# Where the MLP's gate is multiplied in: prepared second weights and sums instead of each pair's results

## The chip, the cores and the metric

The kernel runs on one core of a Trainium2 chip. The metric is device time in microseconds (us) of one launch. The engines named below are PE (TensorE, the matrix products), ACT (ScalarE), DVE (VectorE), POOL (GpSimd) and SP (SyncE, which issues most transfers). Each engine takes its instructions in the order in which they are written; between engines there are only waits on what an instruction reads or overwrites.

## What is computed

A transformer block for 2048 tokens of 640 values with adaptive layer norm: a modulation row is made from `c`, then come linear attention and an MLP. The part that matters is the last line but one, where the row `gb` (640 values, one for each output column) scales the MLP's output:

```
sa, ca, ga, sb, cb, gb = (silu(c) @ w_mod) in six rows of 640
x = x + ga * attention(layernorm(x) * (1 + ca) + sa)
h = layernorm(x) * (1 + cb) + sb
r = relu(h @ w1 + b1)                  # 640 -> 1728
x = x + gb * ((r * r) @ w2 + b2)       # 1728 -> 640
```

Because `gb` scales columns, `gb * (r2 @ w2)` is the same as `r2 @ (w2 * gb)`.

## The kernel before

**Tiles.** Tokens go in 8 pairs j = 0..7 of two 128-token tiles. The hidden axis of 1728 is 14 chunks f (the last one 64 wide), taken two at a time as n = 0..6. A round (j, n) has two halves: `up(j, 2n)` and `up(j, 2n+1)`, each 15 products of 256 columns, and between them the two parts of the `down` products of the round before it. PE works in fp32r; every operand is a rounded high part (ACT copies it, "hi") and a low part (DVE subtracts, `lo`, line 87), and a product is three matmuls (`three`, line 83).

**The chain beside PE.** `up` ends with a relu on ACT (line 1235) and a square on DVE (line 1236). After the second half `split_a` makes the hi (ACT, lines 1259 and 1265) and lo (DVE) parts of the squared chunk pair, and the next round's `down` reads them.

**Second weights.** Pairs 0 and 1 (`PLAIN` = 2) multiply with the plain chunks `W2[f]`. They are prepared by three lists in the same order, `p_load`, `p_hi`, `p_lo`: load a raw row tile by SP (line 994), round it on ACT (line 1001), subtract on DVE (line 1006, by `lo`). W1 and W2 chunks alternate. The first nine entries of the list are rounded during the attention's output stage (j = 1 to 6 there), the other nineteen in the twelve halves of rounds (0, 0) to (0, 5), as many a half as `PREPS` says: 1, 3, 2, 1, 2, 2, 1, 2, 1, 1, 1, 2 (`prep`, line 1450, at lines 1534 and 1585). W2 chunks 2 to 13 are among the nineteen.

**Sums.** From pair 2 on, `down_pair` uses seven products in place of eight, on sums and differences of blocks. The weights' sums are made once, during pair 1 and the start of pair 2: `t_load(n)` loads two raw chunks again, `t_sums(n)` (line 1300) makes five differences on DVE, `t_split(n)` (line 1314) rounds four pieces on ACT, subtracts on DVE and stores three of them to DRAM, from where POOL fetches them in a ring for each later pair. The last pair uses plain chunks again for its last rounds; `plain_load` and `plain_split` (lines 1331 and 1335) prepare a part of two of them anew.

**The gate.** `gb_b` holds `gb` on all partitions. For pairs 0 and 1, `end` (line 1418) multiplies each of four pieces of the accumulated result by it, from PSUM into a row tile. For pairs 2 to 6, `gate` (line 1425) multiplies each finished row tile, 128x640, in place; for pair 7, line 1567 does so before the last products, and `last_downs` (line 1433) multiplies the four pieces that come last into a scratch tile and adds them. `finish` adds the residual and stores.

**What sets the order.** All of it stands in `manual_schedule` blocks for PE, DVE, ACT and POOL: the order on an engine is the order of the text. In the main loop (line 1506) a first half is `up(j, 2n)`, `down` part 0, `layer` (the next pair's layer norm and its transposes, `t2`), `t_split`, `prep`; then `up(j, 2n+1)`, `split_a`, `down` part 1, `prep`, `end`, `layer`, `t_sums`, `t_load`.

Of the kernel before, what the change touches and what calls it, by code (L numbers as in the profile page):

```python
# [8 lines left out]
F32 = mybir.dt.float32  # L9
# [3 lines left out]
ALU = mybir.AluOpType  # L13
AX = mybir.AxisListType

P = 128
S = 2048
D = 640
# [19 lines left out]
PLAIN = 2  # L38
# [12 lines left out]
def kernel(  # L51
# [19 lines left out]
    nc = tc.nc  # L71
# [99 lines left out]
    gb_b = const.tile([P, D], F32, name="gb_b")  # L171
# [224 lines left out]
    def proj(nm, t, between=None):  # L396
        p = pj(f"p{nm}{t}")
        j, i = divmod(t, 2)
        s = slice(i * P, (i + 1) * P)
        for h, (a, b) in enumerate(CUT):  # L400
            terms = []
            for d in range(NC):
                w = W[nm, d]
                terms += three(HT[j][:, d, 0, s], HT[j][:, d, 1, s], w[:, 0, a:b], w[:, 1, a:b])
            at, hook = 0, None
            if between and h == between[0]:
                at, hook = between[1:]
                mm(p[h][:, : b - a], terms[:at], last=False)
                hook()
            mm(p[h][:, : b - a], terms[at:], first=(at == 0))  # L410
        return p
# [299 lines left out]
    for t in range(2, NT - 2):  # L711
        j, i = divmod(t, 2)
# [13 lines left out]
        p = proj("v", t, (1, 0, lambda: t1(j + 1, 4)) if t == NT - 3 else None)  # L726
# [269 lines left out]

    RAW, RAWT, EARLY_ROWS = {}, [], 3

    def prep_hi(k, f):
        w = (W1 if k == "1" else W2)[f]  # L1000
        nc.scalar.activation(w[:, 0], RAW[k, f], AF.Copy)
# [12 lines left out]
    preps = [("1", f) for f in range(EARLY)]  # L1014
# [2 lines left out]
        preps += [("2", f + 1)] * (f + 1 < NF) + [("1", EARLY + f)] * (EARLY + f < NF)  # L1017
    assert len(preps) == 2 * NF
    places = []
    todo = {"load": list(preps), "hi": list(preps), "lo": list(preps)}  # L1020

    def p_load(n=1):
        for _ in range(n):
            if todo["load"]:
                k, f = todo["load"].pop(0)
                prep_load(k, f, places[k, f](f"w{k}_{f}"))

    def p_hi(n=1):
        for _ in range(n):
            if todo["hi"]:  # L1030
                prep_hi(*todo["hi"].pop(0))
# [14 lines left out]
    def load_x1(j):  # L1046
        load_xm(j)
        load_xx(j)
# [16 lines left out]
    def add_x(j, *tiles):  # L1065
        for i in tiles:
            nc.vector.tensor_tensor(XM[j][:, i], XM[j][:, i], XX[j][i], op=ALU.add)
            nc.sync.dma_start(X1[j][:, i], XM[j][:, i])
# [13 lines left out]
    NB = NT // 2  # L1082
# [40 lines left out]
    for j in range(NB):  # L1123
        nxt = j + 1 < NB
        b, c = 2 * j + 5, 2 * j + 6
        late_te = j == 0
        te_at = (0, 1) if 0 < j < 6 else (1, 2)
        if j == 4:
            load_x1(0)
        if j < 5:  # L1130
            p_load()
        if j != 5:
            e_prod(b)
        e_recip(b - 1)
        e_scale(b - 1)
        if j == 5:
            q_chain(KEPT + 3, False)
            add_x(0, 0, 1)
            nc.vector.tensor_tensor(bb, b2s[0], gb_b, op=ALU.mult)
            ln0 = ln_parts(XM[0], "b0")  # L1140
        load_e(b + 2)
        def te(at):
            for i, gs in enumerate((range(3), range(3, NG))):
                if nxt and not late_te and te_at[i] == at:
                    tr_e(j + 1, gs)

        do_wo(j, 0, 0)
        te(0)
        if j == 5:
            exps(EQ[KEPT + 3])  # L1150
            q_sums(KEPT + 3)
            e_prod(b)
        do_wo(j, 0, 1)
        if j == 7:
            t2(0, 0)
            t2(0, 1)
        te(1)
        if j == 5 or j == 6:
            next(ln0)
        if j in SUMS:  # L1160
            q_sums(KEPT + SUMS[j])
        e_prod(c)
        e_recip(b)
        e_scale(b)
        if j in SPREAD:
            q_chain(KEPT + SPREAD[j], False)
        do_wo(j, 1, 0)
        if j == 7:
            t2(0, 2)
            t2(0, 3)  # L1170
        te(2)
        if nxt:
            if late_te:
                tr_e(j + 1, range(NG))
            num(j + 1)
            num_hi(j + 1)
        do_wo(j, 1, 1, 0, 8)
        if j == 7:
            t2(0, 4)
        if not nxt:  # L1180
            do_wo(j, 1, 1, 8, 16)
        if nxt:
            do_wo(j, 1, 1, 8, 11)
            num_lo(j + 1)
            do_wo(j, 1, 1, 11, 16)
        if j in SPREAD:
            exps(EQ[KEPT + SPREAD[j]])
        load_e(c + 2)
        if j == 5:
            next(ln0)  # L1190
        if 1 <= j < 6:
            p_hi()
        if j == 5:
            p_lo(4)
            p_load(4)
        if j == 6:
            p_hi(4)
            p_lo(5)
            p_load(3)
        if j == 7:  # L1200
            p_load(2)
# [5 lines left out]
    p3 = ctx.enter_context(tc.tile_pool(name="p3", bufs=1, reuse_waits="tile"))  # L1207
# [5 lines left out]
    NP = NF // 2  # L1213
# [72 lines left out]
    L, R = slice(0, 384), slice(384, 640)  # L1286
    TR_ = {}
# [12 lines left out]

    def t_sums(n):
        a, b = TR_[n]
        l, r, m = slice(0, 256), slice(384, 640), slice(256, 384)
        if n == NP - 2:
            TR_["end"] = ht("tst_end", 1).rearrange("p d s n -> p (d s n)")
            t = TR_["end"][:, :512].rearrange("p (s n) -> p s n", s=2)
        else:
            t = ring("b", f"tst{n}_b")
        TR_[n, "b"] = t
        for o, x, y in ((a[:, l], a[:, r], a[:, l]), (t[:, 1].bitcast(F32), b[:, r], a[:, r]),  # L1310
                        (b[:, r], b[:, r], a[:, l]), (b[:, m], b[:, m], a[:, m]), (b[:, l], b[:, l], b[:, r])):
            nc.vector.tensor_tensor(o, x, y, op=ALU.subtract)
# [21 lines left out]

    def plain_split(n):
        t, w = W2[2 * n][:, :, R], TR_["plain", n][:, R]
        nc.scalar.activation(t[:, 0], w, AF.Copy)
        lo(t[:, 1], w, t[:, 0])

# [8 lines left out]
    ACC, XR, Y, FIRST = {}, {}, {}, set()  # L1348

    def acc(j, reg):  # L1350

        bank_ = {"3": "3x", "x": "3x", "6": "67", "7": "67"}.get(reg, reg)
        if (j, bank_) not in ACC:
            if len(bank_) == 2:
                ACC[j, bank_] = psC.tile([P, 512], F32, tag=f"p{bank_}", name=f"acc{bank_}_{j}")
            else:
                ACC[j, bank_] = psA.tile([P, 512], F32, tag="pj", name=f"acc{bank_}_{j}", bufs=4)
        t = ACC[j, bank_]
        return (j, bank_), t[:, :384] if len(bank_) == 1 else t[:, 256:] if reg in "x7" else t[:, :256]
# [39 lines left out]
    def add(o, a, b):  # L1399
        nc.vector.tensor_tensor(o, a, b, op=ALU.add)  # L1400

    def by_gate(o, a, c):
        nc.vector.tensor_tensor(o, a, gb_b[:, c], op=ALU.mult)

    def first_combos(j):
        y0, y1 = Y[j] = [row("s2", f"y{j}_{i}") for i in range(2)]
        p = {r: acc(j, r)[1] for r in "1567"}
# [10 lines left out]
    def end(j, r, i, c):  # L1418
        o = Y[j][i][:, c]
        if j >= PLAIN:  # L1420
            add(o, o, acc(j, r)[1])
        else:
            by_gate(o, acc(j, r)[1], c)

    def gate(j, i):
        if j >= PLAIN:
            by_gate(Y[j][i], Y[j][i], slice(0, D))

    def finish(j, i):
        add(Y[j][i], Y[j][i], XR[j, i])  # L1430
        store(j, i)

    def last_downs(j):

        u = p3.tile([P, 8, P], F32, tag="ft", name="end", bufs=2).rearrange("p a b -> p (a b)")
        at = 0
        for regs in ((("3", 0, R), ("x", 1, R)), (("2", 0, L),), (("4", 1, L),)):
            for k in range(2):
                for r, i, c in regs:
                    f = NF - 2 + k  # L1440
                    prod(j, r, block(j, NP - 1, (A11, A12, A21, A22)[2 * i + k]), W2[f], c, k == 1, FS[f])
            for r, i, c in regs:
                m = c.stop - c.start
                t = u[:, at : at + m] if r != "4" else u[:, :m]
                at += m
                by_gate(t, acc(j, r)[1], c)
                add(Y[j][i][:, c], Y[j][i][:, c], t)
                store(j, i, c.start, c.stop)

    def prep(n):  # L1450
        p_hi(n)
        p_lo(n)
        p_load(n)
# [52 lines left out]
    for j in range(NB):  # L1506
# [5 lines left out]
        for n in range(NP):  # L1512
            down = lambda k: prev and (down_plain if plain(*prev) else down_pair)(*prev, k)
            twice = not plain(j, n)
            m = NP * j + n - NP - 1
# [26 lines left out]
                for r, i, c in (("3", 0, R), ("2", 0, L)):  # L1542
                    end(j - 1, r, i, c)
            if n == 1 and j:
                gate(j - 1, 0)
                if j != PLAIN:
                    finish(j - 1, j < PLAIN)
            if n == 1 and j == PLAIN:
                finish(j - 1, 0)
            if n == 2 and j == PLAIN:  # L1550
                t_sums(NP - 2)
            if n == (2 if j > PLAIN else 1) and j:
                gate(j - 1, 1)
            if n == (5, 5, 5, 3)[min(j, 3)]:
                residual(j)
            for i in range(2):
# [5 lines left out]
            if j == NB - 1 and n == 3:  # L1562
                for k in range(NP - LAST, NP - 1):
                    plain_split(k)
            if j == NB - 1 and n == NP - 2:
                for i in range(2):
                    by_gate(Y[j][i], Y[j][i], slice(0, D))
            if j == NB - 1 and n == NP - 1:
                split_a(j, n, (0,))
                for i in range(2):  # L1570
# [94 lines left out]
```

## Time and profile before

| what | value |
|---|---|
| median of 3 runs | 773.87 us (773.56 to 774.21) |
| the profiled execution | 773.97 us |
| its span, first to last instruction | 772.2 us |
| granted TensorE clock, mean | 0.999 |
| DMA | 126.03 MB, mean 163 GB/s |

Times in rows are us from the span's start, "mean ns" is one instruction's duration. A timeline row reads: start, duration, engine, line, operation, output<-input, shape, how many merged, and in brackets the engine's idle time before it with what ended it. The MLP begins at about 394 us: pair 0 lies at 394 to 440, pair 1 at 440 to 488, pairs 2 to 7 after that.

### The profile page before, as it was taken

To read this page: it belongs to the slowest core of one execution; us is meant where nothing else is said; L and a number is where in the kernel's file an instruction comes from. 1 tells how busy PE (TensorE), PEld (TensorE's weight loads), DVE (VectorE), ACT (ScalarE), POOL (GpSimd) and SP (SyncE) were. 2 spreads that over 40 slices of the span, in tenths; PEclk is the share of its full clock that TensorE was granted. 3 is DMA by queue.
4 is the path that set the end of the run, shared out by engine and by line. 5 is a ranking of instruction groups with operands and counts; after the bars stand their busy time and mean duration, and the time that the engine had idled before them with its cause. 6 is when DMAs were issued, how large, how long until landed. Compare 5 with 4: busy or idle time off the path is not lost.

```text
span 772.2 us, 15334 instructions
## 1 busy us (share of the span) xinstructions
PE 764.6 (99%) x5989; PEld 744.1 (96%) x5989; DVE 580.3 (75%) x1057; ACT 443.3 (57%) x995; POOL 145.5 (19%) x301
## 2 busy tenths in 40 slices
PE   9999999999999999999999999999999999999997
PEld 9999999999999979998999999999999999999997
DVE  6598897968999899976266666767767566685666
ACT  5766756667853355656776647456463645546331
POOL 3001101202000255631001001122221313213110
PEclk9999999999999999999999999999999999999999
DMA  9711431512333354232247465997666758667460
GB/s 332 297 65 73 137 103 54 186 37 101 133 103 109 111 160 157 86 105 101 91 137 251 137 212 215 292 320 234 202 178 213 231 178 264 198 185 208 128 171 35
DMA packets 50552, 126.03 MB, mean 163 GB/s; under 512 B 5992, under 2 KB 6760, under 8 KB 50480
## 3 DMA queue, kind: packets, MB, share of 16 engines
q1 hardware_dynamic: 33144, 83.99, 31.7%
q0 software_dynamic: 14752, 35.76, 16.7%
q10 hardware_dynamic: 2583, 5.30, 1.8%
q8 instruction: 47, 0.77, 0.4%
q14 instruction: 26, 0.20, 0.1%
HBM read 95.05 MB, written 29.88 MB: 162 GB/s over the span
## 4 chain that ended last, share of the span: by engine, by line
PE 94%; ACT 2%; DVE 1%; DMA 1%; issue 1%; POOL 0%; SPq 0%; ACTq 0%; POOLq 0%
PE up L77 24%; PE acc L77 17%; PE pwo L77 10%; PE pk L77 8%; PE pq L77 8%; PE pv L77 8%; PE acc3x L77 5%; PE kvp L449 2%; PE te L913 2%; PE tb L356 1%; PE numa L77 1%; PE numb L77 1%; PE numc L77 1%; PE ta L356 1%; PE foldk L279 1%; PE foldq L279 1%
## 5 line engine op out<-in xcount | busy, mean ns | idle before, releaser
L77 PE MATMUL up<-h,w 128*128 128x256 f32 x1640 | 206.5, 278 | 0.2 <-ACT ft L1235 0.2
L77 PEld LDWEIGHTS up<-h,w 128*128 128x128 f32 x1640 | 196.1, 188 | 0.3 <-ACT ft L1235 0.3
L1235 ACT ACTIVATE ft<-up,b_t 128x256 f32<-128x256 f32 x104 | 48.8, 469 | 113.9 <-PE up L77 113.4
L77 PE MATMUL acc<-w,ra 128*128 128x384 f32 x452 | 97.9, 335 | 0.0
L1236 DVE TENSOR_TENSOR ft<-ft 128x256 f32<-128x256 f32 x104 | 44.0, 424 | 50.9 <-ACT ft L1235 49.2
L77 PE MATMUL pwo<-wo,ot 128*128 128x256 f32 (+3 forms) x512 | 81.3, 312 | 0.0
L77 PEld LDWEIGHTS pwo<-wo,ot 128*128 128x128 f32 (+1 forms) x512 | 74.9, 188 | 3.0 <-issue 2.7
L77 PE MATMUL pq<-wq,hT 128*128 128x384 f32 (+1 forms) x480 | 75.4, 312 | 0.0
L77 PEld LDWEIGHTS acc<-w,ra 128*128 128x128 f32 x452 | 72.6, 188 | 0.7 <-DVE ra L87 0.5
L77 PE MATMUL pk<-wk,hT 128*128 128x384 f32 (+1 forms) x480 | 72.7, 308 | 0.0
L77 PEld LDWEIGHTS pq<-wq,hT 128*128 128x128 f32 x480 | 71.2, 188 | 0.8 <-issue 0.2
L77 PE MATMUL pv<-wv,hT 128*128 128x384 f32 (+1 forms) x480 | 71.8, 307 | 0.0
L77 PEld LDWEIGHTS pk<-wk,hT 128*128 128x128 f32 x480 | 70.5, 188 | 0.4 <-issue 0.2
L77 PEld LDWEIGHTS pv<-wv,hT 128*128 128x128 f32 x480 | 70.0, 188 | 0.2
L87 DVE TENSOR_TENSOR ra<-ft,ra 128x384 fp32r<-128x384 f32 (+2 forms) x86 | 36.8, 449 | 32.9 <-ACT ra L1259 20.2
L77 PE MATMUL acc3x<-w,ra 128*128 128x256 f32 x248 | 42.4, 278 | 0.0
L1259 ACT ACTIVATE ra<-ft 128x384 fp32r<-128x384 f32 x48 | 25.2, 525 | 28.4 <-DVE ft L1236 22.4
L1345 POOL DMA_DIRECT2D ring_a<-td_a x34 | 18.2, 536 | 123.6 <-PE acc L77 99.6
L77 PEld LDWEIGHTS acc3x<-w,ra 128*128 128x128 f32 x248 | 39.8, 188 | 0.2 <-DVE ra L87 0.2
L1250 DVE TENSOR_TENSOR ft<-ft 128x128 f32<-128x128 f32 x136 | 33.3, 285 | 1.2
L440 DVE TENSOR_REDUCE sk<-ek 128x64 f32<-128x1280 f32 x16 | 23.7, 1483 | 13.9 <-ACT ek L435 13.4
L477 DVE TENSOR_REDUCE rs_q<-eq 128x64 f32<-128x1280 f32 x16 | 23.7, 1479 | 9.6 <-ACT eq L436 9.6
(260 smaller groups left out, 1413.7 us busy)
## 6 DMA issues: line engine op xcount, KB each, us to landing
ring_c<-td_c POOLq DMA_DIRECT2D x34, 384.0 KB, 4.0
ring_a<-td_a POOLq DMA_DIRECT2D x34, 384.0 KB, 3.9
ring_b<-td_b POOLq DMA_DIRECT2D x34, 256.0 KB, 3.9
esp<-eq SPq DMA_DIRECT2D x12, 640.0 KB, 3.1
el<-esp SPq DMA_DIRECT2D x12, 640.0 KB, 5.0
rw<-in_w SPq DMA_DIRECT2D x23, 320.0 KB, 3.6
wm<-in_w_mod SPq DMA_DIRECT2D x20, 320.0 KB, 3.4
xb<-in_x SPq DMA_DIRECT2D x8, 640.0 KB, 4.0
```

The lines of the kernel that those rows point to most:

```text
L77: nc.tensor.matmul(o, a, b, start=first and i == 0, stop=last and i == len(terms) - 1, skip_group_check=skip,)
L87: (eng or nc.vector).tensor_tensor(out_lo, full, hi.bitcast(F32), op=ALU.subtract)
L279: nc.tensor.matmul(p[g // 3][:, (g % 3) * 120 : (g % 3) * 120 + n], r, bd_t[:120, g * 120 : g * 120 + n], start=True, stop=True,)
L356: nc.tensor.transpose(p[:, i * P : (i + 1) * P], xn[:, i, d * P : (d + 1) * P], ident)
L440: nc.vector.tensor_reduce(s, heads(flat(e)), axis=AX.X, op=ALU.add)
L449: nc.tensor.matmul(kvp[g // 4][64 * c : 64 * c + 64, a : a + 2 * n].rearrange("p (s n) -> p s n", s=2), v[:, u], e[:, :, o : o + n], start ...
L477: nc.vector.tensor_reduce(s, heads(flat(e)), axis=AX.X, op=ALU.add)
L1235: nc.scalar.activation(r, p, AF.Relu, bias=b1_t[:, f : f + 1])
L1236: nc.vector.tensor_tensor(r, r, r, op=ALU.mult)
L1250: nc.vector.tensor_tensor(t[:, o], t[:, a], t[:, b], op=op)
L1259: nc.scalar.activation(a[:, 0, :3], t[:, :3], AF.Copy)
L1345: nc.gpsimd.dma_start(RING[j, n, r], TD[n][r].bitcast(F32R))
```

## The change

A helper `by_gate(t, c)` multiplies columns `c` of a tile by `gb_b` in place on DVE. A fourth list, `p_gate`, runs along with the others and does this to the raw tile of every W2 chunk: for the first nine entries at j = 6 of the attention's output stage, and then at the start of each `prep`. `t_sums` multiplies its two raw chunks, 128x640 each, before the differences, and `plain_split` its piece. In return `gate`, line 1567's loop and the multiplication in `last_downs` go, and `end` copies where it multiplied for pairs 0 and 1.

```diff
+    def by_gate(t, c=slice(0, D)):
+        nc.vector.tensor_tensor(t[:, c], t[:, c], gb_b[:, c], op=ALU.mult)
...
+    def p_gate(n=1):
+        for _ in range(n):
+            if todo["gate"]:
+                k, f = todo["gate"].pop(0)
+                if k == "2":
+                    by_gate(RAW[k, f])
...
         if j == 6:
+            p_gate(9)
             p_hi(4)
             p_lo(5)
             p_load(3)
...
     def t_sums(n):
         a, b = TR_[n]
+        by_gate(a)
+        by_gate(b)
...
     def plain_split(n):
         t, w = W2[2 * n][:, :, R], TR_["plain", n][:, R]
+        by_gate(TR_["plain", n], R)
...
     def end(j, r, i, c):
         o = Y[j][i][:, c]
         if j >= PLAIN:
             add(o, o, acc(j, r)[1])
         else:
-            by_gate(o, acc(j, r)[1], c)
-
-    def gate(j, i):
-        if j >= PLAIN:
-            by_gate(Y[j][i], Y[j][i], slice(0, D))
+            nc.vector.tensor_copy(o, acc(j, r)[1])
...
     def last_downs(j):
...
             for r, i, c in regs:
-                m = c.stop - c.start
-                t = u[:, at : at + m] if r != "4" else u[:, :m]
-                at += m
-                by_gate(t, acc(j, r)[1], c)
-                add(Y[j][i][:, c], Y[j][i][:, c], t)
+                add(Y[j][i][:, c], Y[j][i][:, c], acc(j, r)[1])
                 store(j, i, c.start, c.stop)
...
     def prep(n):
+        p_gate(n)
         p_hi(n)
         p_lo(n)
         p_load(n)
...
-            if n == (2 if j > PLAIN else 1) and j:
-                gate(j - 1, 1)
...
-            if j == NB - 1 and n == NP - 2:
-                for i in range(2):
-                    by_gate(Y[j][i], Y[j][i], slice(0, D))
```

More of the change, by code (lines that the diff above doesn't have):

```diff
@@ L1019 @@
     places = []
-    todo = {"load": list(preps), "hi": list(preps), "lo": list(preps)}
+    todo = {"load": list(preps), "hi": list(preps), "lo": list(preps), "gate": list(preps)}
+    def p_gate(n=1):
[4 more added lines that the diff above has]
+                    by_gate(RAW[k, f])
     def p_load(n=1):
@@ L1400, in add @@
         nc.vector.tensor_tensor(o, a, b, op=ALU.add)
-    def by_gate(o, a, c):
-        nc.vector.tensor_tensor(o, a, gb_b[:, c], op=ALU.mult)
     def first_combos(j):
@@ L1433, in last_downs @@
     def last_downs(j):
-        u = p3.tile([P, 8, P], F32, tag="ft", name="end", bufs=2).rearrange("p a b -> p (a b)")
-        at = 0
         for regs in ((("3", 0, R), ("x", 1, R)), (("2", 0, L),), (("4", 1, L),)):
@@ L1544 @@
             if n == 1 and j:
-                gate(j - 1, 0)
                 if j != PLAIN:
```

## The prediction

> **What bounds the kernel now.** I read the page's busy times, then busy time by stretch, then the timeline of the stretches that the change touches.
>
> ```profile
> PE 764.6 (99%) x5989; PEld 744.1 (96%) x5989; DVE 580.3 (75%) x1057; ACT 443.3 (57%) x995; POOL 145.5 (19%) x301
> 401.60:408.50 6.90, 6.90 (x57) 6.90 (x56) 5.57 (x11) 4.93 (x10) 0.00 (x0) 1.00 0.84 266
> 534.50:580.50 46.00, 46.00 (x364) 45.88 (x364) 31.08 (x76) 23.56 (x51) 11.36 (x23) 1.00 0.71 209
> ```
>
> PE is busy for 764.6 of 772.2 us, and in the MLP (the two stretches: length, then busy PE, PEld, DVE, ACT, POOL, clock) it never stops. So nothing is won by relieving DVE while PE runs, and everything that makes PE wait is lost. Two things count: what the change puts ahead of PE's operands, and what lies behind PE's last product.
>
> **Prices.** Groups by line and form:
>
> ```profile
> L498 DVE TENSOR_TENSOR rwo<-rwo,ga_b 128x640 f32<-128x640 f32 x5 | 4.1, 817 | 0.0
> L1403 DVE TENSOR_TENSOR y<-y,gb_b 128x640 f32<-128x640 f32 x12 | 9.7, 816 | 0.0
> L293 DVE TENSOR_SCALAR wm<-wm,cs 128x640 f32<-128x640 f32 x4 | 2.2, 546 | 0.0
> L1403 DVE TENSOR_TENSOR y<-acc3x,gb_b 128x256 f32<-128x256 f32 x4 | 1.7, 420 | 0.9 <-PE acc3x L77 0.9
> L821 DVE COPY zb<-z 128x240 f32<-128x240 f32 x2 | 0.7, 402 | 0.6 <-ACT zb L823 0.6
> ```
>
> L498 is the added form itself: a weight row tile times a broadcast row, in place, 0.82 us. The change adds 14 such for W2, 12 in six sums and 2 of 256 columns (0.42): 26 x 0.82 + 2 x 0.42 = 22.2 us. It removes 12 x 0.82 = 9.8 (pairs 2 to 7) and four pieces at the end. DVE has more work than before. The eight pieces that are now copied cost about the same (402 ns for 240 columns against 420 for 256); between half and equal, I take equal, and either is hidden, since PE is full there.
>
> **W2's first two gates** stand in the attention's last stage, and the row there shows DVE idle for long:
>
> ```profile
> 386.19 1.56 DVE L87 TENSOR_TENSOR w<-rawt,w 128x640 fp32r<-128x640 f32 x2 [12.95 <-ACT w L1001]
> ```
>
> Two gates (1.6 us) fit into 12.95: nothing. Without that cover they would delay ACT by as much.
>
> **The other twelve gates**, in rounds (0,0) to (0,5), are the step that decides. Timeline where the MLP starts:
>
> ```profile
> 395.76 3.90 PE L77 MATMUL up<-h,w 128*128 128x256 f32 x33
> 396.30 0.47 ACT L1235 ACTIVATE ft<-up,b_t 128x256 f32<-128x256 f32 x1 [0.79 <-PE up L77]
> 396.67 0.73 ACT L1001 ACTIVATE w<-rw 128x640 fp32r<-128x640 f32 x1
> 396.80 0.43 DVE L1236 TENSOR_TENSOR ft<-ft 128x256 f32<-128x256 f32 x1 [1.11 <-ACT ft L1235]
> 397.43 0.83 DVE L87 TENSOR_TENSOR w<-rw,w 128x640 fp32r<-128x640 f32 x1 [0.20 <-ACT w L1001]
> 398.00 0.47 ACT L1235 ACTIVATE ft<-up,b_t 128x256 f32<-128x256 f32 x1 [0.60 <-PE up L77]
> 398.50 0.43 DVE L1236 TENSOR_TENSOR ft<-ft 128x256 f32<-128x256 f32 x1 [0.25 <-ACT ft L1235]
> 398.96 0.53 ACT L1259 ACTIVATE ra<-ft 128x384 fp32r<-128x384 f32 x1 [0.49 <-DVE ft L1236]
> 399.52 0.76 DVE L87 TENSOR_TENSOR ra<-ft,ra 128x384 fp32r<-128x384 f32 x2 [0.59 <-ACT ra L1259]
> 399.54 1.03 PE L77 MATMUL acc<-w,ra 128*128 128x384 f32 x3
> ```
>
> Today ACT rounds a W2 chunk (396.67) at once, while DVE squares. Now the rounding waits for the gate, the gate stands behind the square on DVE, and the next relu stands behind the rounding on ACT. By these rows: square to 397.23, gate 397.2 to 398.0, rounding 398.0 to 398.7, relu 398.65 (before 398.00), subtraction 398.8 to 399.5, square at 399.5 (before 398.50). Split and subtraction follow 1.0 later, and PE, which before just got its operand (399.54), waits **1.0**.
>
> I carry both queues on in this way, row by row: a row starts when the one before it on its engine leaves (0.08 to 0.10 before its end, as adjacent rows show) and 0.03 after what it reads is ready. ACT waits again for gate 3 (0.8, behind the split's subtractions) and gate 4 (1.8, behind three subtractions and a square, of which some replaces an old wait). The split of round (0,1) then comes 3.3 late; gates 5, 6 and 7 bring the chain to 4.5 at round (0,3); gate 8 is covered by two layer norm rows on ACT; gates 9 and 10 add 1.5 each (5.95, then 7.4). PE is late by that less the slack at each meeting:
>
> ```profile
> 405.38 0.76 DVE L87 TENSOR_TENSOR ra<-ft,ra 128x384 fp32r<-128x384 f32 x2 [0.59 <-ACT ra L1259]
> 406.73 0.68 PE L77 MATMUL acc<-w,ra 128*128 128x384 f32 x3
> ...
> 419.69 0.76 DVE L87 TENSOR_TENSOR ra<-ft,ra 128x384 fp32r<-128x384 f32 x2 [0.59 <-ACT ra L1259]
> 420.41 0.68 PE L77 MATMUL acc<-w,ra 128*128 128x384 f32 x3
> ...
> 426.96 0.76 DVE L87 TENSOR_TENSOR ra<-ft,ra 128x384 fp32r<-128x384 f32 x2 [0.59 <-ACT ra L1259]
> 427.25 0.76 PE L77 MATMUL acc<-w,ra 128*128 128x384 f32 x3
> 427.66 0.91 ACT L1481 ACTIVATE xm<-xm,nbb,sqb 128x640 f32<-128x640 f32 x1
> 429.08 0.60 PE L356 MATMUL tb<-ident,xm 128*128 128x128 f32 x4
> ...
> 436.29 0.55 ACT L367 ACTIVATE xx<-tb,cols_b 128x256 f32<-128x256 f32 x1
> 436.91 0.42 PE L356 MATMUL tb<-ident,xm 128*128 128x128 f32 x2
> ```
>
> The first subtraction of a pair of rows takes 0.56, and PE's third matmul, two of 0.17 after the first, is the one that reads it. Round (0,1): ready 405.94, read at 407.07, slack 1.1, PE late 3.3 - 1.1 = 2.2. Round (0,3): ready 420.25, read 420.75, 4.5 - 0.5 = 4.0. Round (0,4): 427.52 against 427.59, 5.95 - 0.1 = 5.85. The next pair's transposes wait for the normed rows: 428.57 against 429.08, 7.4 - 0.5 = **6.9**. Gate 11 and, back to back, gates 12 and 13 then hold ACT before the transposes' copies: 2.9 more, and the last transposes (436.91) have no slack behind the copy (436.84): **9.8**.
>
> **The sums.** Two gates put 2 x 0.74 = 1.5 (spaced as the pairs of rows above) before each. The first three sums lie ahead of work for which PE does not wait yet; the fourth and fifth don't:
>
> ```profile
> 482.61 0.76 DVE L87 TENSOR_TENSOR ra<-ft,ra 128x384 fp32r<-128x384 f32 x2 [0.59 <-ACT ra L1259]
> 483.37 0.69 PE L77 MATMUL acc<-w,ra 128*128 128x384 f32 x3
> ...
> 486.96 0.42 DVE L87 TENSOR_TENSOR h<-xx,h 128x256 fp32r<-128x256 f32 x1
> 488.24 1.86 PE L77 MATMUL up<-h,w 128*128 128x256 f32 x15
> ```
>
> Round (1,5): ready 483.17, read 483.71, slack 0.5: 1.5 - 0.5 = 1.0. Pair 2's first `up` needs the last normed column, 487.38 against 488.24: slack 0.86, the chain 2.05 later than PE (1.5 from the fifth sum, the rest carried from the fourth): 1.2. The sixth sum and `plain_split` stand where PE's operands are ready a half earlier: nothing. Lost in all: 9.8 + 1.0 + 1.2 = **12.0 us**. SP's loads and stores and POOL's fetches move with the chain; the raw rows are issued two or three halves ahead.
>
> **The end.**
>
> ```profile
> 765.09 1.90 PE L77 MATMUL acc<-w,ra 128*128 128x384 f32 x10
> 765.29 0.42 DVE L1403 TENSOR_TENSOR end<-acc3x,gb_b 128x256 f32<-128x256 f32 x1 [0.83 <-PE acc3x L77]
> ...
> 766.20 3.28 SPq L1397 DMA_DIRECT2D out<-y  x4
> 768.53 0.56 DVE L1400 TENSOR_TENSOR y<-y,end 128x384 f32<-128x384 f32 x1
> ```
>
> PE ends at 766.99, but four multiplications and four additions keep DVE until 769.09. Without the multiplications the last addition starts when PE is done: 767.0 + 0.56 = 767.58, **1.5 less**. The four stores keep 0.3 or more between them.
>
> Sum: +12.0 - 1.5 = +10.5. On the profiled execution's 773.97 (0.10 above the median of the runs) that is **784.5 us**, slower by 1.4%.
>
> **Bounds.** If a gate cost only what the cheapest 640-wide multiplication does (546 ns), the same queues give PE 8 late, 780.5. If each handover between ACT and DVE takes 0.06 in place of 0.03, it is 13 to 14, 786.5.
>
> **Rivals.**
> A, not slower: the gates find DVE idle ahead of their place. The first row of the square shows 1.11 of idle time just before it, over the 0.82 of a gate; if the gate ran there, before the square, ACT would never wait. It decides at one point: whether a gate is queued before or behind the row that waits for the relu. Behind, by the text; ahead, only the end counts: 772.5. Chance 0.05.
> B, fewer waits: ACT's backlog covers some gates as it covers gate 8, and the sums' are hidden: PE late 3 to 6, 776 to 780. Chance 0.08.
> C, more: the sums leave DRAM late, so POOL's first fetches for pair 2 miss their products, or a raw row lands after its gate; one landing of about 4 us once: 787 to 789. Chance 0.06.
> D, the clock falls: PE now stops six to nine times. In the stretches above the granted clock is 1.00 with PE never idle, so before shows nothing of stops. Were it halved for as long as the longest replayed stop, 2.9 us, after each of two such stops, another 3 us would go: 787.5. Chance 0.02. The Trainium skill, TensorE: Matmul & The Clock Gate, Part 1: The HAM clock gate, says that the clock halves after an idle window of about 3.4 us; by that rule no single stop here is long enough, and the sum would stay; the trace of before has no idle window of that length in the MLP to test it on.
> The forecast, 780.5 to 787: 0.79.
>
> **Chances.** A measurement of this kernel tells about 0.2% (1.5 us) from no change. A falls on that edge: faster 0.02, same 0.03; the rest is slower, 0.95. The range 780.5 to 787 leaves out A, B and part of C and D, about 0.2.
>
> **What would show it.** Each W2 rounding on line 1001 in pair 0 should have idle time before it, ended by a DVE multiplication of the raw row; PE's waits, almost none now, should name `ra` and the transposes, ten to twelve us in all before 500 us; from pair 2 on PE should be as full as before, and the span's end come 1.5 us sooner after PE's last product. It is wrong if PE stays full through pair 0, or if the added time lies behind 510 us.

## The result, and the profile after

| | before | after |
|---|---|---|
| median of six runs each | 773.76 us (773.54 to 774.21) | 787.12 us (784.77 to 787.45) |
| the profiled execution | 773.97 us | 787.07 us |
| its span | 772.2 us | 785.4 us |
| granted clock, mean | 0.999 | 0.998 |

The change makes the kernel slower: the ratio is 1.0167, 95% interval 1.0155 to 1.018. Five of the six runs of after lie at 786.92 to 787.45 us with a mean clock of 0.997 or 0.998; the sixth, with 1.000, took 784.77. That difference is part of the story below. (The 0.999 of before is no sign of it: its clock shows 0.50 only behind PE's last product, for the last 1.79 us.)

The page of after, busy time of each engine; then the stretches of it (length, busy PE, PEld, DVE, ACT, POOL, clock):

```profile
PE 771.3 (98%) x5989; PEld 746.9 (95%) x5989; DVE 588.7 (75%) x1069; ACT 444.1 (57%) x995; POOL 146.3 (19%) x301
```

```profile
401.60:408.50 6.90, 6.49 (x52) 6.29 (x51) 5.86 (x9) 3.58 (x7) 0.00 (x0) 1.00 0.70 216
...
594.50:776.00 181.50, 181.50 (x1431) 181.16 (x1430) 115.25 (x288) 85.56 (x189) 39.14 (x76) 1.00 0.65 189
```

The stretch in pair 0, full in before, now has 0.41 us in which PE stands; from 594.5 us on PE is full again. DVE's share of the span is 75% as before, so the share shows nothing of the loss. Where the MLP starts, the timeline of after:

```profile
396.99 0.43 DVE L1247 TENSOR_TENSOR ft<-ft 128x256 f32<-128x256 f32 x1 [1.11 <-ACT ft L1246]
397.33 0.82 DVE L1000 TENSOR_TENSOR rw<-rw,gb_b 128x640 f32<-128x640 f32 x1
398.18 0.74 ACT L1004 ACTIVATE w<-rw 128x640 fp32r<-128x640 f32 x1 [1.23 <-DVE rw L1000]
398.83 0.46 ACT L1246 ACTIVATE ft<-up,b_t 128x256 f32<-128x256 f32 x1
...
399.70 0.42 DVE L1247 TENSOR_TENSOR ft<-ft 128x256 f32<-128x256 f32 x1
...
400.15 0.52 ACT L1270 ACTIVATE ra<-ft 128x384 fp32r<-128x384 f32 x1 [0.86 <-DVE ft L1247]
...
400.73 1.03 PE L77 MATMUL acc<-w,ra 128*128 128x384 f32 x3 [0.88 <-ACT ra L1270]
```

The gate (L1000) starts behind the square, the rounding (L1004) waits 1.23 us for it, the next relu comes behind the rounding, and PE waits 0.88. The waits of after between 384 and 520 us (total, times, longest) show how often:

```profile
ACT w L1004 <- DVE rw L1000: 12.0, 10, 1.7
...
PE acc L77 <- ACT ra L1270: 4.6, 5, 1.3
...
PE tb L356 <- ACT xx L367: 2.1, 1, 2.1
...
PE tb L356 <- ACT xm L1482: 0.8, 1, 0.8
```

**PE's lateness.** From the two timelines I took the start of every cluster of `up` products, after less before, and took off the difference at the MLP's first product (0.19 us). One number a place then says how much PE has lost by there:

| `up` of | forecast | after | `w2_gates_only` | `sum_gates_only` | `gate_time_no_wait` | `gate_one_half_earlier` |
|---|---|---|---|---|---|---|
| (0,3) | 1.0 | 1.01 | 1.01 | 0.01 | 0.12 | 0.41 |
| (0,5) | 2.2 | 2.43 | 2.40 | 0.01 | 0.45 | 1.45 |
| (0,9) | 4.0 | 4.04 | 4.01 | 0.01 | 0.81 | 1.60 |
| (0,11) | 6.9 | 6.70 | 6.70 | 0.03 | 1.16 | 3.23 |
| (0,13) | 9.8 | 9.60 | 9.61 | 0.03 | 1.59 | 4.69 |
| (1,0) | 9.8 | 11.21 | 9.63 | 0.03 | 1.59 | 4.69 |
| (1,9) | 9.8 | 11.57 | 9.63 | 0.36 | 2.83 | 5.02 |
| (1,11) | 9.8 | 12.00 | 9.67 | 0.81 | 3.25 | 5.43 |
| (1,13) | 10.8 | 13.01 | 9.67 | 1.85 | 4.31 | 6.49 |
| (2,1) | 12.0 | 13.91 | 9.67 | 2.75 | 5.20 | 7.38 |
| (2,8) | 12.0 | 14.43 | 9.91 | 3.53 | 5.98 | 7.87 |

Behind (2,8) only two columns still grow: `gate_time_no_wait` to 6.27 in pair 3, `sum_gates_only` to 3.81 at (6,8). The span's difference closes with it: 14.43 + 0.19 - 1.5 (the end, below) = 13.1, against 785.4 - 772.2 = 13.2 of the rounded spans.

**A stop, and what followed.** Between (0,13) and (1,0) PE loses 1.6 us for which no wait is listed. The timeline of after at the last transposes:

```profile
446.68 0.44 PE L356 MATMUL tb<-ident,xm 128*128 128x128 f32 x2 [2.15 <-ACT xx L367]
446.87 2.12 PE L77 MATMUL up<-h,w 128*128 128x256 f32 x10
```

and the stretches of after around it (PE's busy time is the second number, the clock stands third from the end; a step of it from 1.00 to 0.50 is called a fall below):

```profile
443.89:447.30 3.41, 1.26 (x10) 1.07 (x9) 2.78 (x5) 3.35 (x7) 0.00 (x0) 1.00 0.22 46
447.30:450.72 3.42, 3.42 (x17) 3.42 (x16) 2.91 (x7) 1.99 (x6) 0.00 (x0) 0.50 0.95 320
450.72:453.00 2.28, 2.28 (x20) 2.28 (x20) 1.15 (x4) 0.42 (x1) 0.00 (x0) 1.00 0.07 26
```

After a stop of 2.15 us PE counts as fully busy for 3.42 us, but at half clock, and does half the work: ten `up` products took 2.12 us, where the same row of `w2_gates_only`, shown below, has 1.42.

**The sums and the end.** In pair 1 the waits in after's timeline are

```profile
496.25 1.04 PE L77 MATMUL acc<-w,ra 128*128 128x384 f32 x3 [0.53 <-ACT ra L1270]
...
504.78 0.62 PE L77 MATMUL acc<-w,ra 128*128 128x384 f32 x2 [0.48 <-DVE ra L87]
```

and behind PE's last product

```profile
779.71 1.90 PE L77 MATMUL acc<-w,ra 128*128 128x384 f32 x10
...
780.77 0.56 DVE L1414 TENSOR_TENSOR y<-y,acc 128x384 f32<-128x384 f32 x1
781.64 0.55 DVE L1414 TENSOR_TENSOR y<-y,acc 128x384 f32<-128x384 f32 x1 [0.31 <-PE acc L77]
```

From the start of the last ten products to the end of the last addition before took 769.09 - 765.09 = 4.00 us, after 782.19 - 779.71 = 2.48: 1.5 less.

### The profile page after: what moved, and what is told of

It is laid out like the page before. It is cut to its first block, busy times and chain, and to the rows that moved or that the text cites. A ratio compares the mean times of both kernels' runs of the same rounds, so it can differ in the third digit from the quotient of the medians.

```text
span 785.4 us, 15329 instructions
## 1 busy us (share of the span) xinstructions
PE 771.3 (98%) x5989; PEld 746.9 (95%) x5989; DVE 588.7 (75%) x1069; ACT 444.1 (57%) x995; POOL 146.3 (19%) x301
## 4 chain that ended last, share of the span: by engine, by line
PE 85%; ACT 6%; DVE 5%; issue 2%; DMA 1%; POOL 1%; ACTq 0%; POOLq 0%; DVEq 0%
PE up L77 19%; PE acc L77 15%; PE pwo L77 10%; PE pk L77 8%; PE pq L77 8%; PE pv L77 8%; PE acc3x L77 3%; PE kvp L449 2%; PE te L913 2%; PE numa L77 1%; PE tb L356 1%; PE foldk L279 1%; PE numb L77 1%; DVE ft L1247 1%; PE numc L77 1%
## 5 line engine op out<-in xcount | busy, mean ns | idle before, releaser
L77 PE MATMUL acc<-w,ra 128*128 128x384 f32 x452 | 101.0, 341 | 5.2 <-ACT ra L1270 4.6
L1247 DVE TENSOR_TENSOR ft<-ft 128x256 f32<-128x256 f32 x104 | 44.1, 424 | 55.6 <-ACT ft L1246 54.6
```

Source lines behind the costliest of these rows:

```text
L77: nc.tensor.matmul(o, a, b, start=first and i == 0, stop=last and i == len(terms) - 1, skip_group_check=skip,)
L1247: nc.vector.tensor_tensor(r, r, r, op=ALU.mult)
```

## The experiments

The theory: in pair 0 it is not DVE's time that costs, but that a rounding on ACT waits for a gate issued just before it, with the next relu behind the rounding. The main rival: DVE's extra time itself.

**One part at a time: the second weights' gates without the sums' gates.** `w2_gates_only`, after with

```diff
     def t_sums(n):
         a, b = TR_[n]
-        by_gate(a)
-        by_gate(b)
...
     def plain_split(n):
         t, w = W2[2 * n][:, :, R], TR_["plain", n][:, R]
-        by_gate(TR_["plain", n], R)
```

> The changed kernel without the multiplications in t_sums and plain_split: from pair 2 on the sums' products lack the gate, so the output differs. Chain theory (time is lost because ACT's rounding waits for the gate on DVE and the relu waits behind the rounding): pair 0 keeps its loss of 9.6 us and the stretch at half clock (1.6) behind the 2.2 us stop, pair 1 loses nothing, the end keeps its gain of 1.5: 773.8 + 11.2 - 1.5 = 783.5 us, 782 if the clock does not fall. Rival, the amount of DVE work, wherever it stands: 14 of 27 gates, about half of the 14.4 us lost: 773.8 + 7.5 - 1.5 = 780.

Measured 781.66 us (781.18 to 782.44), ratio 1.0102 [1.0087, 1.0117]. Pair 0 is as in after (column above), pair 1 adds nothing. The same stop is there, but the clock stayed; timeline and a stretch of this kernel:

```profile
445.81 0.44 PE L356 MATMUL tb<-ident,xm 128*128 128x128 f32 x2 [2.15 <-ACT xx L367]
446.00 1.42 PE L77 MATMUL up<-h,w 128*128 128x256 f32 x10
```

```profile
446.41:449.82 3.41, 3.41 (x29) 3.41 (x28) 2.90 (x7) 2.02 (x6) 0.00 (x0) 1.00 0.95 321
```

In the 3.4 us that begin 0.6 us behind the stop PE ran 29 matmuls at clock 1.00, in after 17 at 0.50. So the length of a stop alone doesn't decide.

**The other part alone.** `sum_gates_only`, after with

```diff
-                k, f = todo["gate"].pop(0)
-                if k == "2":
-                    by_gate(RAW[k, f])
+                todo["gate"].pop(0)
```

> The changed kernel without the multiplication of W2's raw rows: the plain products and the unsummed products lack the gate, so the output differs. Chain theory: pair 0 as before the change, pairs 1 and 2 lose 2 to 3 us, the end gains 1.5: 774.3 to 775.5 us. Rival, the amount of DVE work: 13 of 27 gates, 773.8 + 7 - 1.5 = 779.

Measured 775.83 us (774.79 to 776.77), ratio 1.0025 [1.0016, 1.0034]. The sums cost PE 3.5 us, from (1,9) on, and 0.3 more at (6,8), less 1.5 at the end; the median lies 0.3 above the range expected.

**DVE's time without ACT's wait.** `gate_time_no_wait` puts a DVE operation of the same length at the gate's place, which reads the raw row and writes elsewhere:

```diff
-                    by_gate(RAW[k, f])
+                    nc.vector.tensor_reduce(ce, RAW[k, f].rearrange("p (a b) -> p a b", b=P), axis=AX.X, op=ALU.add)
```

> The changed kernel with each of the 14 W2 multiplications replaced at its place by a DVE reduction that reads the same raw row and writes five columns that nothing reads (about 0.81 us by the row of L309 before, as long as the gate): W2 is not gated, the output differs. DVE is as busy as in the changed kernel, but ACT's rounding no longer waits. Chain theory: the same replay without that wait gives 1.4 us lost in pair 0, 2 to 3 in pairs 1 and 2, no stop long enough for the clock, the end 1.5 sooner: 775.5 to 777 us. Rival, the amount of DVE work: 785 to 787 as the changed kernel.

Measured 778.33 us (777.73 to 778.51), ratio 1.0057 [1.0042, 1.0071]. The timeline of this kernel where the one of after is shown above:

```profile
396.51 0.73 ACT L1004 ACTIVATE w<-rw 128x640 fp32r<-128x640 f32 x1
396.64 0.43 DVE L1247 TENSOR_TENSOR ft<-ft 128x256 f32<-128x256 f32 x1 [1.10 <-ACT ft L1246]
396.98 0.81 DVE L1030 TENSOR_REDUCE ce<-rw 128x5 f32<-128x640 f32 x1
...
399.48 1.03 PE L77 MATMUL acc<-w,ra 128*128 128x384 f32 x3
```

The rounding starts at 396.51 beside the relu's tail, not at 398.18, and the products come with no wait listed. Pair 0 loses 1.6 us instead of 9.6, and 0.9 more at the start of pair 1 (a split's 64 rows behind DVE). DVE's time is worth at most 2.5 us; the other 7.1 of the 9.6 are ACT's wait. The time is 1.3 us above the 775.5 to 777 expected: the 0.9 was not in that sum, and the sums' gates cost more than the 2 to 3 us put down for them.

**The gate a half ahead of its rounding.** `gate_one_half_earlier`, after with `p_gate` behind `p_lo` for the next half's entries:

```diff
         if j == 7:
             p_load(2)
+            p_gate()
...
     def prep(n):
-        p_gate(n)
         p_hi(n)
         p_lo(n)
+        p_gate(AHEAD.pop(0) if AHEAD else 0)
...
+    AHEAD = [3, 2, 1, 2, 2, 1, 2, 1, 1, 1, 2]
```

> The same instructions and the same result as the changed kernel, but in pair 0 each W2 gate stands one half earlier on DVE, behind that half's subtractions, so that it is done when ACT comes to the rounding. Chain theory: the replay gives 3.9 us lost in pair 0 (DVE's own time still delays squares and splits), 2 to 3 in pairs 1 and 2, no fall of the clock, the end 1.5 sooner: 778 to 779.5 us. Rival, the amount of DVE work: 785 to 787, unchanged.

Measured 781.0 us (780.21 to 781.15), ratio 1.0093 [1.0076, 1.011]. ACT's waits for gates fall from 12.0 us to 3.1, by the list of waits of this kernel:

```profile
ACT w L1004 <- DVE rw L1000: 3.1, 3, 1.5
...
PE acc L77 <- ACT ra L1271: 2.8, 5, 1.2
```

Half of pair 0's loss goes (4.69 is left of 9.60). The gates now stand ahead of squares and subtractions instead (one at 398.06 holds the square that follows until 398.80). The mean clock was 0.999 to 1.0. The time is 1.5 us above the 778 to 779.5 expected: pair 0 lost 4.7 in place of 3.9, and the sums' gates again more than 2 to 3.

**The gates on POOL.** `gates_on_pool` is the last kernel with `by_gate` on `nc.gpsimd` for the second weights, ten of the twelve sum gates and the pieces of `plain_split`, the latter two kinds one step ahead of their use.

```diff
-        nc.vector.tensor_tensor(t[:, c], t[:, c], gb_b[:, c], op=ALU.mult)
+        nc.gpsimd.tensor_tensor(t[:, c], t[:, c], gb_b[:, c], op=ALU.mult)
...
```

> The changed kernel's result with the gates on POOL: the W2 gates one half earlier, as in gate_one_half_earlier, but as POOL instructions; ten of the twelve sum gates and the last pair's two pieces on POOL half a round before they are needed, the sixth sum's two stay on DVE. No trace yet shows such a row on POOL. Chain theory: if one takes under about 2.5 us, they are ready in time and neither DVE nor ACT has more to do than before, so PE is as full as before and the end comes 1.5 us sooner: 772.3 to 773 us. Rival, more gates anywhere cost about as much as they take: no better than 778.

Measured 789.88 us (788.86 to 791.85), ratio 1.0212 [1.0197, 1.0227]: the expectation missed. The group of the gates, then the timeline of this kernel at its longest stop:

```profile
L1000 POOL TENSOR_TENSOR rw<-rw,gb_b 128x640 f32<-128x640 f32 x13 | 22.2, 1723 | 32.0 <-DMA rw<-in_w 19.0 <-DVE w L87 11.5 <-DMA xm<-a 1.4
```

```profile
424.46 7.12 POOL L1000 TENSOR_TENSOR rw<-rw,gb_b 128x640 f32<-128x640 f32 x4
...
426.31 1.79 DVE L1248 TENSOR_TENSOR ft<-ft 128x256 f32<-128x256 f32 x1
...
428.02 2.16 DVE L87 TENSOR_TENSOR w<-rw,w 128x640 fp32r<-128x640 f32 x1
430.11 1.75 DVE L1248 TENSOR_TENSOR ft<-ft 128x256 f32<-128x256 f32 x1
431.89 0.52 ACT L1271 ACTIVATE ra<-ft 128x384 fp32r<-128x384 f32 x1 [3.91 <-DVE ft L1248]
...
432.46 1.28 PE L77 MATMUL acc<-w,ra 128*128 128x384 f32 x3 [3.97 <-ACT ra L1271]
```

One gate takes 1723 ns there, against 819 on DVE. But PE's stop is not a wait for a gate: ACT waits 3.91 us for a square on DVE, and while POOL multiplies, DVE's own rows are long: two squares of 1.79 and 1.75 us in place of 0.42, a subtraction of 2.16 in place of 0.82. The last of them ends at 431.86, 0.28 behind the last gate's end. Of the kernel's 104 squares the 94 with no gate of POOL beside them took 410 to 435 ns; of the other ten, five took 1352 to 1793. ACT's rows beside the gates keep their length (0.46, 0.74, 0.91). Over the whole kernel DVE has 26 instructions fewer than in `gate_one_half_earlier`, some 20.5 us of gates, and is busy for 589.9 us against 588.4. So the gates left DVE's queue and lengthened its other rows by about as much as they had taken. Against what is said at the start, waits on operands are then not all that links two engines, and the theory did not have this link; what POOL and DVE share is not shown by these rows. Two of this kernel's stops also halved the clock (see below), from 432.85 and from 480.64 us on.

**The end by itself.** `before_end_ungated` is before without the four multiplications of `last_downs`.

> The kernel before with the four multiplications in last_downs left out, so the last pair's output lacks the gate in part. It measures the end alone. If the last addition then starts when PE is done, the time falls by 1.5 us, to 772.4. Rival: the last store's landing or SP's issue sets the end, and nothing is won.

Measured 772.29 us (771.67 to 772.82) against 773.92, ratio 0.9978 [0.997, 0.9987]: 1.6 us, the end's term.

**Stops of a set length.** The clock was left open. Four kernels hold ACT up, in before, so that PE stops once a pair in a stretch that is full otherwise:

```diff
+    STOPS = {2: 13, 3: 16, 4: 18, 5: 21, 6: 23}
...
+            for _ in range(STOPS.get(j, 0) if n == 2 else 0):
+                nc.scalar.activation(ones, ones, AF.Copy)
             if j >= PLAIN and n == 0:
                 down(1)
             split_a(j, n, (0, 1) if (j, n) != (NB - 1, NP - 1) else (1,))
...
```

> The kernel before, with one stop of PE in each of pairs 2 to 6, of growing length: ahead of the split in the third round ACT copies a constant tile onto itself 13, 16, 18, 21 and 23 times, about 0.2 us each by the spacing of its shortest rows, against a slack of 1.4. The result is unchanged. Stops of about 1.2, 1.8, 2.2, 2.8 and 3.2 us, 11 in all: 785 us if the clock holds. If the clock halves whenever a stop is longer than some length, the rows behind the longer ones show 0.5 and those behind the shorter 1.0, alike in every run, 1.7 us more for each. If it depends on where a stop falls in time, runs of the same kernel differ.

> As stops_graded, with 18 copies, a stop of about 2.2 us, in each of pairs 2 to 6: 785 us if the clock holds. If a length decides, all five stops have the same consequence: clock 1.0 behind all, or 0.5 behind all (1.7 us each, 793). If the place in time decides, some are followed by 0.5 and some are not, and the runs of this one kernel spread by steps of about 1.7 us.

Measured 805.09 us and 803.14 us, ratios 1.0405 [1.0389, 1.0421] and 1.0377 [1.0363, 1.0391]. The lengths planned were missed: by the idle times in the timelines the stops were 2.04, 3.06, 3.74, 4.76 and 5.45 us in `stops_graded` and five of 3.74 in `stops_equal`, and all ten were followed by clock 0.50. That answered nothing on stops of about 2 us, except that in `stops_graded` the clock fell at 512.70, 563.90, 615.1, 666.3 and 720.9: 51.2, 51.2, 51.2 and 54.6 apart, 15, 15, 15 and 16 times 3.413 us. So two more, with shorter stops and a long one in pair 7:

```diff
-    STOPS = {2: 13, 3: 16, 4: 18, 5: 21, 6: 23}
+    STOPS = {2: 13, 3: 13, 4: 13, 5: 13, 6: 13, 7: 18}
```

> The kernel before, with ScalarE held up ahead of the split of round 2: 13 copies of a constant tile onto itself in pairs 2 to 6, 18 in pair 7 (the result stays the same). In stops_graded 13 such copies stopped PE for 2.04 us and 18 for 3.74, so here five equal stops of about 2.04 us are wanted, close to the 2.15 us of the changed kernel, and a long one at the end that shows the clock's phase. In stops_graded and stops_equal all ten stops (2.04 to 5.45 us) were followed by the clock 0.50, and the falls of stops_graded stand at 512.70, 563.90, 615.1, 666.3 and 720.9: apart by 51.2, 51.2, 51.2 and 54.6 us, which is 15, 15, 15 and 16 times 3.41 us. Theory A: the clock is set at fixed instants 3.41 us apart, by how much PE stood in the stretch before; then some of the five 2.04 us stops, those that an instant cuts so that neither part is over about half of 3.41 us, leave the clock at 1.00, and those inside one stretch give 0.50 for about 3.3 us (1.6 us lost): 1 to 4 falls of five, at instants that fit one grid of 3.41 us, time 793 to 798 us. Theory B, the length alone decides (2.04 us is enough): five falls of five, about 800 us, and then the kernel with only the second weights' gates, whose 2.15 us stop left the clock alone, has another reason. Theory C, chance from run to run: falls that fit no grid.

Measured 797.55 us, ratio 1.0311 [1.0281, 1.0341]. Of five equal stops of 2.04 us, the first, second and fourth were followed by 0.50, the third and fifth were not. The stretches of this kernel on a grid of 3.41 us laid through its falls (512.02, 563.22, 662.20 and 761.19, apart by 15, 29 and 29 times 3.413):

```profile
508.61:512.02 3.41, 1.37 (x13) 1.18 (x11) 0.12 (x1) 3.16 (x11) 0.52 (x1) 1.00 0.95 282
512.02:515.43 3.41, 3.41 (x12) 3.26 (x13) 3.38 (x11) 2.17 (x6) 0.00 (x0) 0.50 0.21 83
...
607.60:611.01 3.41, 2.68 (x24) 2.48 (x22) 0.41 (x1) 3.09 (x11) 1.06 (x2) 1.00 0.94 257
611.01:614.42 3.41, 2.10 (x11) 1.81 (x12) 2.09 (x6) 2.87 (x9) 0.26 (x1) 1.00 0.39 131
614.42:617.83 3.41, 3.41 (x30) 3.41 (x30) 1.61 (x5) 2.84 (x8) 1.70 (x5) 1.00 0.59 177
```

The first stop lies inside one stretch (PE busy 1.37 of 3.41), and the next stretch runs at 0.50. The third is cut by an edge (0.73 us in one, 1.31 in the next), and the clock stays. In PE's lateness a 2.04 us stop cost 2.6 us without a fall (third and fifth) and 3.9 to 4.15 with one: a fall costs 1.3 to 1.6 us.

`stops_short_graded`, with `{1: 10, 2: 11, 3: 12, 4: 12, 5: 14, 6: 14, 7: 18}`:

> The same as stops_short_equal with 10, 11, 12, 12, 14 and 14 copies in pairs 1 to 6 and 18 in pair 7: stops of about 1.0, 1.4, 1.7, 1.7, 2.4, 2.4 and 3.7 us by the 0.34 us a copy of stops_graded (13 copies 2.04, 18 copies 3.74). Theory A (fixed instants 3.41 us apart, the share of the stretch before in which PE stood decides, with a bound near a half): the stops of 1.0 and 1.4 us never make the clock fall, those of 1.7 hardly (they fill a half at most), those of 2.4 mostly (at least 1.2 lies on one side, and over 1.7 in it unless the cut is near the middle). Theory B (length alone, with a bound somewhere from 1.0 to 2.04 us): all stops over the bound fall and none under it, whatever their place; two equal stops then never differ. Theory D: the bound is lower than a half and stops of 1.0 and 1.4 us fall too, which would make the single 0.4 us and 0.8 us waits of pair 0 in a row matter. Time 787 to 796 us.

Measured 797.71 us (796.65 and 798.78, clocks 0.996 and 0.992), ratio 1.0313 [1.0279, 1.0346], above the 787 to 796 expected; the stops cost PE more than their length here too. Its stretches, on the grid of its own falls:

```profile
559.24:562.65 3.41, 1.72 (x15) 1.52 (x14) 0.23 (x1) 3.16 (x11) 0.53 (x1) 1.00 1.03 311
562.65:566.06 3.41, 3.41 (x24) 3.11 (x24) 2.90 (x8) 2.93 (x8) 0.84 (x2) 1.00 0.23 85
...
654.81:658.22 3.41, 2.32 (x21) 2.12 (x19) 0.05 (x1) 3.09 (x11) 1.06 (x2) 1.00 1.00 269
658.22:661.63 3.41, 2.12 (x11) 1.83 (x12) 2.11 (x6) 2.87 (x9) 0.26 (x1) 1.00 0.29 99
661.63:665.04 3.41, 3.41 (x31) 3.41 (x30) 1.64 (x5) 2.86 (x8) 1.72 (x5) 1.00 0.59 159
706.01:709.42 3.41, 1.10 (x5) 0.81 (x6) 1.12 (x4) 3.18 (x10) 0.26 (x1) 1.00 0.53 171
709.42:712.83 3.41, 3.41 (x16) 3.41 (x14) 2.01 (x5) 2.25 (x5) 1.15 (x3) 0.50 0.38 117
```

Two stops of 2.38 us differ: the one cut at 658.22 leaves the clock alone, the one that left PE 1.10 us busy in a stretch halves it. A stop of 1.70 us that fills half of one stretch (busy 1.72 of 3.41) does not. So theory A stands: the clock is set on a grid of 3.41 us, by the stretch just past, and the bound lies between 50% idle (no fall) and 60% (fall). The two runs' different clocks say that the grid's place isn't fixed to the program.

This can be tried on the kernel whose stop of 2.15 us left the clock alone. In `w2_gates_only` the clock falls only behind PE's last product, at 778.96 us, which shows its grid: 98 times 3.4133 us earlier an edge lies at 444.45, inside the 2.15 us stop (443.66 to 445.81). The stretches of this kernel:

```profile
441.04:444.45 3.41, 2.58 (x15) 1.89 (x14) 2.98 (x6) 2.04 (x5) 0.00 (x0) 1.00 0.34 96
444.45:447.86 3.41, 2.05 (x16) 2.05 (x17) 2.38 (x7) 3.29 (x8) 0.00 (x0) 1.00 0.66 199
447.86:451.28 3.42, 3.42 (x29) 3.42 (x28) 3.11 (x8) 1.44 (x5) 0.00 (x0) 1.00 0.56 185
```

The edge leaves 0.8 us of the stop in one stretch and 1.36 in the next, 40% idle, and the clock stays, as theory A has it. In after all 2.15 us lie in one stretch.

**A gain at the end without the loss?** `last_chunks_gated` is before, with hidden chunks 12 and 13 of the second weights loaded again in pair 7, gated and split anew, each rounding a round behind its gate, and the multiplications of `last_downs` gone. It leaves a part of the computation out: the accumulators that it adds at the end also hold the rounds before the last, which no gate reaches, so it is no version to use, and only its time is read.

```diff
+    def last_split(f):
+        t, w, m = TR_["last", f], W2[f], FS[f]
+        nc.scalar.activation(w[:, 0], t, AF.Copy)
+        lo(w[:m, 1], t[:m], w[:m, 0])
...
-                by_gate(t, acc(j, r)[1], c)
-                add(Y[j][i][:, c], Y[j][i][:, c], t)
+                add(Y[j][i][:, c], Y[j][i][:, c], acc(j, r)[1])
```

> The kernel before, changed at one place only: the last two hidden chunks (12 and 13) of the second weights are loaded again in pair 7 once pair 6 has used them, multiplied by the gate there, rounded and subtracted again over the old ones, in halves in which DVE's rows of before show 1.2 to 2.0 us of idle time; each rounding stands a round behind its gate. The four multiplications in last_downs go. The theory of this study: DVE's time beside a full PE costs nothing as long as ACT is not made to wait for a gate just issued, so PE's lateness stays below 0.2 us and the end gains what before_end_ungated gained (772.29 against 773.89, -1.6): about 772.3 us, ratio 0.998. Rival 1, DVE's extra 3.2 us in pair 7 delay squares or splits: PE late by 0.3 to 1.5 in pair 7, 772.6 to 773.8. Rival 2, the loads in pair 7 come between other transfers of SP and make the residual rows late: 774 or more.

Measured 773.24 us (771.95 to 773.61) against 774.15, ratio 0.9986 [0.9977, 0.9995]. PE's lateness is the same 0.25 us at every `up` of pair 7: two gates, two roundings and two subtractions there make PE no later. The 772.3 expected was missed by 0.9: five of the eleven runs took 771.95 to 772.85 us, the profiled one (772.6) among them, and six 773.24 to 773.61; no trace shows where those six lost it. The timeline of this kernel:

```profile
737.40 0.82 DVE L1418 TENSOR_TENSOR w2g<-w2g,gb_b 128x640 f32<-128x640 f32 x1 [1.58 <-DMA w2g<-in_w]
...
742.91 0.82 DVE L87 TENSOR_TENSOR w<-w2g,w 128x640 fp32r<-128x640 f32 x1
```

A version that keeps the result would need accumulators of its own for the last round and four more pieces on DVE before the end; it wasn't tried. No version found here beats before.

## Why the prediction was right, and where its sum was short

The forecast was 784.5 us in a range of 780.5 to 787.0; the median is 787.12, a tenth above the range's end. The sign, the places and most of the size are those forecast; 2.6 us are missing from the sum, 1.6 of them the clock's and 1.0 the sums'.

- *PE bounds, and only its waits count*: right. DVE's added time alone cost 2.5 us at most (`gate_time_no_wait`), and made PE no later in pair 7 (`last_chunks_gated`).
- *Pair 0, 9.8*: right, 9.60, and place by place within 0.25 (table). The cause is the one named: with ACT's wait gone 1.6 is left, with the gate half a round ahead 4.7. Rival A, a gate in DVE's idle time ahead of its place, is out: at 397.33 the gate stands behind the square. B (fewer waits, 3 to 6 us) is out too.
- *The first two gates free*: right as far as it can be told; the MLP begins 0.19 us later in after, and in the traces of `stops_short_equal` and `before_end_ungated`, which change nothing ahead of it, 0.44 later and 0.55 earlier.
- *The sums, 2.2*: the mechanism right, the size short: 14.43 - 11.21 = 3.2 in after, 3.5 alone. The 1.0 at round (1,5) came as forecast (12.00 to 13.01 in the table). The step that failed is "the first three sums lie ahead of work for which PE does not wait yet": 0.36 and 0.43 were lost earlier ((1,9) and (1,11)), with ACT's split late. And the 1.2 that I put on pair 2's first `up` fell on the 64-row split of round (1,6) instead (504.78, 0.9). The last 0.5, at (2,4) and (2,8), lie where POOL's first ring fetches for pair 2 meet their products, rival C's place at an eighth of its price. In `sum_gates_only` the waits name a ring's transfer there (PE `acc` for DMA `ring_a<-td_a`, 0.4 us), in after none does, and 0.24 comes at (2,4) in `w2_gates_only` too; so that link is seen in one kernel and argued for after.
- *The end, -1.5*: right; 1.5 by the timelines, 1.6 by `before_end_ungated`.
- *No term for the clock*: this is the step that failed. Rival D had a chance of 0.02, at 3 us; it came in one stop, for 1.6 us of PE's lateness. Five of after's six runs show the lower mean clock (only 3.8 us follow PE's last product in after, at most some 2 of them at 0.50, which alone would leave the mean at 0.999: an estimate), and the one with 1.000 took 784.77, the forecast to 0.3 us. That closeness is in part luck: the profiled execution's 787.07 less the clock's 1.6 is 785.5, and the sums' missing 1.0 is in it. I had "by that rule no single stop here is long enough"; the runs showed that a stop of 2.04 us is long enough if it lies inside one stretch of the grid. In after the stretch 443.89 to 447.30 held the whole 2.15 us stop, PE busy 1.26 of 3.41, or 63% idle. In the profiled execution of `w2_gates_only` an edge of the grid cuts the same stop, and the clock stays. That after falls in five of six runs and `w2_gates_only` in none of four is then a matter of where the grid lies in each run; whether the shares are chance is not settled by so few.

The Trainium skill, TensorE: Matmul & The Clock Gate, Part 1: The HAM clock gate, says that the window of about 3.4 us runs free, without regard to the kernel's start. The distances of the falls here, multiples of 3.413 us, agree. It also says that the halving comes after an idle window; here a window 60% idle was enough, and one of 50% was not, so the measurement narrows the rule: what counts is how much of one window a stop fills, not that it is longer than the window.

## What to carry to other kernels

Price an added operation by the queue it is put into, not by the engine's idle share: ask which instruction of another engine waits for it, and what stands behind that one. Twelve gates of 0.82 us cost at most 2.5 us as DVE time and 9.6 as something ACT had to wait for; on POOL, busy for only 19% of the span before, they made DVE's own rows longer and cost more still. An engine's idle time is no spare time until a trace shows that the other engines' rows keep their length beside it. And when a change makes a full PE stop, add to each stop of about 2 us and more some 1.5 us for the clock, with a chance that grows with its length (here four of six stops of 2.04 us were followed by a fall, and all of 3 us and more).

## What the runs showed of the hardware

- The granted clock is set on a grid of 3.413 us that isn't tied to the program's start. A stretch in which PE stood for 2.0 us or more was followed by 3.41 us at 0.50; one with 1.70 us was not; two stops of 2.38 us differed by where the grid cut them.
- PE counts as busy at half clock: only the clock column and the longer rows (2.12 us against 1.42 for ten products) show it, the busy share doesn't.
- A 128x640 fp32 product of two row tiles took 1723 ns on POOL, in the mean of 13, and 819 on DVE.
- Beside such a product on POOL, a DVE square of 128x256 took up to 1793 ns in place of 410 to 435, and ACT's rows kept their length (`gates_on_pool`).
